# One delta-rule attention and two expert layers on one core: all pieces of a step at other places, W's expanded copies by DMA and ScalarE, two token tables

## The chip, the cores and the metric

The kernel runs on one core of one Trainium2 chip. A core has five engines that run their own instruction lists in order: TensorE (PE, matmuls; PEld is its loading of weights), VectorE (DVE), ScalarE (ACT), GpSimd (POOL) and SyncE (SP), which here only issues DMAs. They wait for one another by semaphores. Sixteen DMA engines move data between the device memory and the on-chip memory, or inside the latter. The metric is the device time of one execution in microseconds, as the median of several runs.

## The reference

```
attention (4 batches, 8 heads, 768 tokens, 48 wide), for each token t:
    y[t]   = q[t] @ state
    state += beta[t] * outer(kn[t], v[t] - kn[t] @ state)        kn = k / |k|
x   = y as [3072 tokens, 384]
x   = sum over 4 experts e:  p[:, e] * (relu(x @ w1[e]) @ w2[e])           # 384 -> 1024 -> 384, dense
out = gate * (relu(x @ v1[e*]) @ v2[e*]),  e* = the best of 8 experts for each token
```

Inputs and output are float32. The first layer needs every expert for every token, the second one expert for each token.

## The kernel before

**Numbers.** Matmuls run on pairs of 16-bit floats: a value is split into a high part (written by ACT) and a low part (the rest, by DVE or POOL), and each product is three matmuls.

**Attention** is cut into 12 steps of 64 tokens for all 32 heads (two halves x of 16 heads). In a step the keys are normed (`norm_squares` to `norm_apply`), split (`split_k`), transposed by a DMA (`turn_k`), summed into the right operand KQ (`sum_k`) and multiplied with themselves (`gram_k`) and with the queries (`gram_q`). A 32 x 32 triangular system for each head is inverted on DVE in lanes, with 31 pivots (`inverse`, lines 396 and 400), turned back (`from_lanes`) and split into TB (`split_t`, ACT L421 and DVE L422). Then come `rest` (the part of v that the state predicts), the side R, `solve_z`, `solve_y` and `solve_w`; their results, in the tile Ws, are spread with gaps into WB by `expand(0)` and `expand(1)` (line 497, four DVE copies each). `state` and `keep` update the state, `outputs` and `columns` (lines 142, 143) make the next x, transposed, in `xT`.

**Dense layer.** While attention step s runs, the dense layer works on the tokens of step s - 1. It has 16 pieces for each step; `Dense.first` (line 834; L838 and L839 make H) and `Dense.second` (line 856; after every fourth piece its sum leaves PSUM, L864 or L866). Between them are 32 **half-slots** for each step: an even one stands behind `first` of the next piece, an odd one behind `second`.

**The order by hand.** Nothing is scheduled by a tool. The tables `SLOTS` and `SECOND` (the latter for attention step 1) say in which half-slot of its dense step each piece of an attention step is written down, with negative numbers for the dense step before. `route_pieces` (the choice of the expert, half-slots 2 to 26) and `w_split` (the weights of the second layer, split and stored to the device memory image `wimg`, lines 1029 to 1033) have their own slots, and `DENSE` and `KINDS` those of the dense weights in dense step 0: a kind A, B or C says which engines split a chunk (A: ACT, ACT, POOL; B: ACT, DVE; C: ACT, POOL, POOL). Every engine gets its instructions in the order in which the half-slots are written down, and so does the SP queue with its DMAs. Two places that matter:

```python
at[16i ...]:  hidden(i + 1);  at[2 * i];  second(i);  at[2 * i + 1]      # dense piece i
SLOTS = dict(load_k=-4, norm=(-2, -1, 0, 1), ..., sum_k=(-5, -1), gram_k=(-4, 0), ..., out=27, ...)
```

So the keys of step s + 1 are loaded in half-slot 28 of one dense step and squared (L178, on ACT) in half-slot 30, two behind.

**The first step** (`begin`) has nothing to lie beside and is written down as a list of its own, before dense step 0. **Token numbers** of the tokens that go to an expert are scattered by POOL (line 1116) into one table `ids` in device memory, two scatters a step. **The sparse layer** is a tail of 27 tiles of 128 tokens: gather, transpose, `hidden` (L1295), `emit` (L1312), scatter. Its first list is read by `list_a`, and `phase_a` starts the gathers and the loads of the first three tiles' weights (L1267) in half-slot 18 of the last dense step.

Of the kernel before, what the change touches and what calls it, by code (L numbers as in the profile page):

```python
# [26 lines left out]
DENSE = dict(w=(0, 0, 1, 1, 2, 3, 3, 4, 4, 5, 6, 7, 8, 9, 10, 11, 13, 14, 15, 16, 17, 18, 20, 21, 22, 23, 24, 25, 26), r=16, t=20, e=22, c=26, i=21, p=5, load=0, keep=1)  # L27


class Attention:  # L30
# [3 lines left out]
    def __init__(self, ctx, tc, q, k, v, beta, ident, pp, xt_pool, late):  # L34
# [32 lines left out]
        self.clear(self.WB[:, 0:1])  # L67
        self.clear(self.KB0[1])
# [153 lines left out]
    def split_wide(self, s, x, low):  # L222
        KM = self.KM[:, 8 * x:8 * x + 8]
        hi, lo = (self.keys(s)[x][:, l].rearrange("p u (h c) -> p u h c", h=2)[:, :, :, 0:48] for l in range(2))
        self.nc.scalar.activation(out=hi, in_=KM, func=AF.Copy)
        low.tensor_tensor(out=lo, in0=KM, in1=hi, op=ALU.subtract)

    def split_q(self):
        self.split_q_hi()
        self.split_q_lo()  # L230

    def split_q_hi(self):
        Qv = self.Q.rearrange("p (g h) d -> p g h d", h=2)
        for h in range(2):
            self.nc.scalar.activation(out=self.QT[:, 0, :, h, 0:48], in_=Qv[:, :, h], func=AF.Copy, scale=64.0)

    def split_q_lo(self):
        nc = self.nc
        Qv = self.Q.rearrange("p (g h) d -> p g h d", h=2)
        for h in range(2):  # L240
            nc.vector.scalar_tensor_tensor(out=self.QT[:, 1, :, h, 0:48], in0=Qv[:, :, h], scalar=64.0,
                                           in1=self.QT[:, 0, :, h, 0:48], op0=ALU.mult, op1=ALU.subtract)

    def split_q_whole(self):
        nc, Q = self.nc, self.Q
# [118 lines left out]
    def split_p(self, x):  # L364
        nc = self.nc
        src = self.P32[:, 8 * x:8 * x + 8]
        nc.scalar.activation(out=self.PT[x][:, 0], in_=src, func=AF.Copy)
        self.low.tensor_tensor(out=self.PT[x][:, 1], in0=src, in1=self.PT[x][:, 0], op=ALU.subtract)
# [44 lines left out]
    def split_t(self, between=None):  # L413
        nc, TR = self.nc, self.pr
        if between:
            between()
        for q in range(4):
            b = slice(32 * q, 32 * q + 32)
            hi, lo = (self.TB[b, :, l, b].rearrange("c p (i y) -> c i p y", y=2) for l in range(2))
            src = TR[b].rearrange("c i (p y) -> c i p y", y=2)  # L420
            nc.scalar.activation(out=hi, in_=src, func=AF.Copy)  # L421
            nc.vector.tensor_tensor(out=lo, in0=src, in1=hi, op=ALU.subtract)  # L422
# [67 lines left out]
    def expand(self, f):  # L490

        for q in range(4):
            r, g, c = slice(32 * q, 32 * q + 32), q // 2, 48 * (q % 2)
            par = f ^ g
            dst = self.WB[r, :, 0:1536].rearrange("p l (u e) -> p l u e", e=96)[:, :, par:16:2, c:c + 48]
            src = self.Ws[r, par]
            self.nc.vector.tensor_copy(dst, src)
# [53 lines left out]
    def pieces(self, s):  # L551
        two = range(2)
        st = {}
# [19 lines left out]
        if s > 1:  # L573
            for x in two:
                at(P["split_k"][x], lambda x=x: self.split_k(s, x))
                at(P["turn_k"][x], lambda x=x: self.turn_k(s, x))
                at(P["sum_k"][x], lambda x=x: [self.sum_k(x, l) for l in two])
                at(P["gram_k"][x], lambda x=x: self.gram_k(x))
            at(P["split_q"], self.split_q)
# [7 lines left out]
        for n in range(4):  # L587
            f = self.expand_s if s > 1 else self.expand_d
            at(P["expand_s"][n], lambda n=n, f=f: f(*divmod(n, 2)))
        at(P["to_lanes"], lambda: self.scale_lanes(s))  # L590
# [15 lines left out]
        at(P["y"], self.save_z, self.solve_y, self.solve_yl)  # L606
        at(P["y"] + 1, lambda: self.expand(0))
        at(P["w"], self.solve_w)
        at(P["w"] + 1, lambda: self.expand(1))
# [18 lines left out]
    def begin(self, loads, parts):  # L628
        nc, two = self.nc, range(2)
        K0, K1 = self.K0, self.K1  # L630
        for x in two:
            self.blank(self.KBs[x], 2)
        loads(0)
        self.twin_beta()
        self.load_v(0)
        self.blank(self.AO, 2)
        loads(1)
        self.blank(self.TB, 4)
        loads(2)
        self.blank(self.WB[:, 1:2], 1)  # L640
        for x in two:
            self.blank(self.SB[x], 2)
        self.blank(self.KBs[2], 2)

        self.K = K0
        self.units("out", bufs=2)
        sq = self.sq = self.wk.tile([128, 16, 48], F32, name="ksq", tag="wb")
        nc.vector.tensor_tensor(out=sq, in0=K0, in1=K0, op=ALU.mult)
        self.norm_root()
        self.norm_scale()  # L650
        rm = self.norm_heads(nc.vector, self.r0)
        for x in two:
            self.norm_wide(nc.vector, K0, x, rm)
        for x in two:
            self.split_wide(0, x, nc.vector)
        for x in two:
            for l in two:
# [877 lines left out]
```

## Time and profile before

| | us |
|---|---|
| median of 3 runs (lowest, highest) | 1322.87 (1321.1, 1325.64) |
| the profiled execution | 1319.7 |
| its span, first to last instruction | 1317.9 |
| first step of attention, alone | 0 to 61.3 |
| dense step 0 | 61.3 to 173.6 |
| dense steps 1 to 9 | 173.6 to 954 |
| dense steps 10 and 11 | 954 to 1090 |
| tail of 27 tiles | 1090 to 1318 |

| engine | busy us | share of the span |
|---|---|---|
| PE | 1149.0 | 87% |
| PEld | 880.9 | 67% |
| DVE | 840.1 | 64% |
| ACT | 638.7 | 48% |
| POOL | 450.4 | 34% |

How to read the rows below: a row of a view of windows gives, for a stretch, its length, for each engine the busy time (and number of instructions), then the granted TensorE clock (1.00 is 2.4 GHz, 0.50 is 1.2 GHz), the mean busy share of the DMA engines and their GB/s. A row of waits says who waited for whom: total us, times, longest. A row of the timeline has the start, the length, the engine, the line and the tiles, and in brackets the idle time before it and what ended that. A row of groups has the busy time, the mean ns of one, and the idle time before.

### The profile page before, as it was taken

The numbers are of one execution on the slowest core, as the hardware profiler recorded it, in microseconds if no ns is written. First come the engines' busy times: TensorE is split into PE (matmuls) and PEld (weight loads), VectorE is DVE, ScalarE is ACT, GpSimd is POOL, SyncE is SP. The second block draws the span as 40 slices with busy tenths as digits, with TensorE's granted clock in tenths as the row PEclk, the third lists the DMA queues.
The fourth block names the chain that finished last, engine by engine and source line by source line (L and its number), as shares of the span: only waits on it lengthen the run. The fifth ranks groups of instructions, "written<-read, shape, count | busy, mean of one in ns | idle before, by whom it ended". The sixth has DMA issues, their size and how long they took to land. (4 is left out here: it accounts for less than half of the span.)

```text
span 1317.9 us, 32914 instructions
## 1 busy us (share of the span) xinstructions
PE 1149.0 (87%) x12906; PEld 880.9 (67%) x12906; DVE 840.1 (64%) x2898; ACT 638.7 (48%) x1248; POOL 450.4 (34%) x436
## 2 busy tenths in 40 slices
PE   3477699798798898988988979879899999999997
PEld 3355577566576676766766757657677777878876
DVE  8776778588577676886776768767777344212221
ACT  6665655355464455555554646555564314222221
POOL 5466732332334224323243233423441022222221
PEclk8688999999899899999998999989999999999999
DMA  9981244725524446254364463444532157796960
GB/s 224 220 194 17 45 99 115 104 66 137 81 64 117 81 115 105 71 132 87 91 108 80 128 116 90 113 81 121 113 94 73 25 157 230 247 282 181 342 171 27
DMA packets 249504, 163.00 MB, mean 124 GB/s; under 512 B 196271, under 2 KB 230908, under 8 KB 249344
## 3 DMA queue, kind: packets, MB, share of 16 engines
q1 hardware_dynamic: 243600, 150.77, 48.6%
q0 software_dynamic: 4656, 9.87, 2.4%
q8 instruction: 104, 1.70, 0.6%
q14 instruction: 56, 0.46, 0.1%
q10 hardware_dynamic: 1088, 0.20, 0.1%
HBM read 142.52 MB, written 35.80 MB: 135 GB/s over the span
## 5 line engine op out<-in xcount | busy, mean ns | idle before, releaser
L856 PEld LDWEIGHTS <-H 128*128 128x128 f16 x2304 | 224.9, 100 | 217.6 <-issue 44.1
L856 PE MATMUL po<-W,H 128*128 128x384 f16 x1728 | 324.2, 338 | 50.9 <-ACT H L838 37.1
L834 PE MATMUL ph<-xT,W 128*128 128x256 f16 x2808 | 336.3, 275 | 7.5 <-POOL W L819 6.0
L834 PEld LDWEIGHTS <-W 128*128 128x128 f16 x2808 | 272.7, 99 | 52.5 <-POOL W L819 7.4
L839 DVE SCALAR_TENSOR_TENSOR H<-ph,H 128x512 f16<-128x512 f32 x192 | 131.5, 688 | 161.9 <-ACT H L838 160.8
L1031 POOL TENSOR_TENSOR wso<-wst,wso 128x768 f16<-128x768 f32 x64 | 105.1, 1642 | 281.6 <-ACT wst L1030 259.7
L838 ACT ACTIVATE H<-ph 128x512 f16<-128x512 f32 x192 | 112.7, 592 | 154.3 <-PE ph L834 153.3
L1300 DVE SCALAR_TENSOR_TENSOR H<-ph,H 128x512 f16<-128x512 f32 x54 | 37.2, 690 | 151.3 <-ACT H L1299 151.3
L856 PE MATMUL po<-Wlate,H 128*128 128x384 f16 x576 | 102.6, 332 | 18.5 <-DVE acc L866 18.5
L1295 PEld LDWEIGHTS <-slot 128*128 128x128 f16 x1944 | 110.7, 98 | 3.8 <-issue 0.5
L1295 PE MATMUL ph<-xt,slot 128*128 128x128 f16 x1944 | 113.1, 219 | 0.2 <-DMA xt<-g 0.2
L400 DVE TENSOR_TENSOR tt<-tt,pr 128x60 f32<-128x60 f32 (+34 forms) x660 | 110.7, 210 | 0.7
L1312 PE MATMUL po<-slot,H 128*128 128x384 f16 x648 | 110.0, 326 | 0.6 <-DVE H L1300 0.6
L396 DVE TENSOR_TENSOR pr<-tt,KQ 128x60 f32<-128x60 f32 (+34 forms) x660 | 108.4, 202 | 0.8
L1312 PEld LDWEIGHTS <-H 128*128 128x128 f16 x648 | 62.1, 98 | 39.1 <-DVE H L1300 0.9
L1317 POOL DMA_INDIRECT out_dram<-ob,idx x27 | 27.3, 1011 | 166.6 <-ACT ob L1316 129.6
L834 PE MATMUL ph<-xT,Wlate 128*128 128x256 f16 x648 | 78.8, 276 | 3.8 <-ACT Wlate L815 2.5
L215 POOL TENSOR_TENSOR KB<-Kr,KB 32x384 f16<-32x384 f32 x80 | 76.7, 958 | 5.8 <-ACT KB L214 1.3
L362 POOL TENSOR_TENSOR AO<-O,AO 32x256 f16<-32x256 f32 x48 | 32.8, 684 | 128.7 <-ACT AO L361 126.7
L1029 ACT ACTIVATE wso<-wst 128x768 f16<-128x768 f32 x64 | 53.3, 833 | 44.1 <-DMA wimg<-wso 42.1
L834 PEld LDWEIGHTS <-Wlate 128*128 128x128 f16 x648 | 61.6, 99 | 12.7 <-ACT Wlate L815 2.9
L1299 ACT ACTIVATE H<-ph 128x512 f16<-128x512 f32 x54 | 32.2, 597 | 77.0 <-PE ph L1295 75.6
(308 smaller groups left out, 1615.2 us busy)
## 6 DMA issues: line engine op xcount, KB each, us to landing
slot<-wimg SPq DMA_DIRECT2D x108, 768.0 KB
wst<-in_moe_w_dram SPq DMA_DIRECT2D x65, 384.0 KB
wimg<-wso SPq DMA_DIRECT2D x64, 384.0 KB
xb<-xr SPq DMA_DIRECT2D x48, 98.0 KB
Qr<-in_q_dram SPq DMA_DIRECT2D x24, 192.0 KB
Vr<-in_v_dram SPq DMA_DIRECT2D x96, 48.0 KB
W<-in_moe_w_dram SPq DMA_DIRECT2D x11, 384.0 KB
Kr<-in_k_dram SPq DMA_DIRECT2D x84, 48.0 KB
```

The lines of the kernel that those rows point to most:

```text
L215: self.low.tensor_tensor(out=KB[r, 1, :, 64 * h:64 * h + 48], in0=src, in1=hi, op=ALU.subtract)
L396: nc.vector.tensor_tensor(out=p, in0=t[:, :, j:j + 1].to_broadcast([128, m, j]), in1=AT[:, j, 0:j].unsqueeze(1).to_broadcast([128, m, j]), ...
L400: nc.vector.tensor_tensor(out=t, in0=t, in1=p, op=ALU.subtract)
L834: nc.tensor.matmul(ph[:, i], w1[:, a, k, 128 * i:128 * i + 128], xT[:, b, k], start=(n == 0), stop=(n == 8))
L838: nc.scalar.activation(out=H[:, 0], in_=ph, func=AF.Relu)
L839: nc.vector.scalar_tensor_tensor(out=H[:, 1], in0=ph, scalar=0.0, in1=H[:, 0], op0=ALU.max, op1=ALU.subtract)
L856: nc.tensor.matmul(po[t], H[:, a, i, 128 * t:128 * t + 128], w2[:, b, i], start=(f == 0 and i == 0 and n == 0), stop=(f == 3 and i == 1 an ...
L1029: self.nc.scalar.activation(out=o[:, 0], in_=t, func=AF.Copy, scale=scale)
L1031: self.nc.gpsimd.tensor_tensor(out=o[:, 1], in0=t, in1=o[:, 0], op=ALU.subtract)
L1295: nc.tensor.matmul(ph[:, i], w[:, a, k, 128 * (i % 2):128 * (i % 2) + 128], xt[:, 3 * b + k], start=(m == 0), stop=(m == 8))
L1300: nc.vector.scalar_tensor_tensor(out=H[:, 1], in0=ph, scalar=0.0, in1=H[:, 0], op0=ALU.max, op1=ALU.subtract)
L1312: nc.tensor.matmul(po, H[:, a, i], w[:, b, i % 2], start=(q == 0 and i == 0 and m == 0), stop=(q == 1 and i == 3 and m == 2))
```

## The change

What is computed stays. Other places (half-slots) for nearly every piece, other engines for some, and a second table:

- The tables `SLOTS` and `SECOND`, `DENSE`, `KINDS` (with a kind D: all on POOL), the slots of the routing pieces and of `w_split` are replaced.
- `expand(0)` of steps 1 to 11 is done by eight DMAs from the SP queue, `expand(1)` by four ScalarE copies. The state's expanded copies `SB` go by DMA for half 0 (two DMAs for each of two pieces) and stay on ACT for half 1.
- The low part of the keys of half 1 moves from POOL to DVE.
- `begin` becomes a list of named pieces in the order of the text `ORDER`.
- The two scatters of a step go to a table each; `list_a` gathers from both, and `list_b` takes the smaller number.
- `phase_a` moves from half-slot 18 to 21 of the last dense step.

```diff
-SLOTS = dict(load_k=-4, norm=(-2, -1, 0, 1), split_k=(-10, -7), turn_k=(-8, -5), sum_k=(-5, -1), gram_k=(-4, 0), to_lanes=1, split_g=(1, 2), split_q=-4, turn_q=-3, gram_q=(5, 6), split_p=(6, 7), expand_s=(8, 10, 12, 14), init=2, pivots=(2, 3, 3, 2, 2, 3, 3, 3, 3, 3, 2, 2), from_lanes=14, split_t=15, rest=(16, 17), z=19, y=21, w=23, state=25, keep=25, out=27, load_q=16, load_v=23)
-SECOND = dict(SLOTS, to_lanes=0, split_g=(8, 10), gram_q=(9, 10), split_p=(11, 12), expand_s=(5, 6, 7, 8), init=1, pivots=(2, 2, 3, 2, 3, 2, 3, 2, 3, 2, 3, 2, 2), from_lanes=14, split_t=15, rest=(12, 15), z=17, y=19, w=21, state=23, keep=23, out=25, load_k=0, load_q=16, load_v=22, norm=(13, 15, 18, 18))
-HEAD = dict(loads=(2, 5, 7, 15, 23))
-KINDS = "AAABABACABACABACABACBACBABCABABA"
+SLOTS = dict(load_k=-6, load_q=16, load_v=36, norm=(2, 2, 3, 4), split_k=(-24, -7), turn_k=(-14, -5),
+             sum_k=(-5, -1), gram_k=(-2, 0), to_lanes=0, scale=0, split_g=(1, 4), split_q=(-4, -4), turn_q=0,
+             gram_q=(5, 6), split_p=(8, 7), expand_s=(8, 10, 12, 14), init=5, pivots=(4, 6, 3, 3, 5, 5, 2, 3, 0),
+             from_lanes=13, split_t=15, rest=(15, 17), z=19, save=19, y=21, e0=22, w=24, e1=24, state=25, keep=25,
+             out=28)
+SECOND = dict(load_k=0, load_q=18, load_v=34, norm=(14, 17, 17, 18), split_k=(-14, -7), turn_k=(-11,
+              -7), sum_k=(-5, -1), gram_k=(-2, 0), to_lanes=0, scale=1, split_g=(7, 11), split_q=(-4, -4), turn_q=-3,
+              gram_q=(9, 10), split_p=(12, 13), expand_s=(4, 3, 7, 8), init=1, pivots=(4, 0, 4, 0, 4, 1, 4, 4, 1, 2,
+              5, 2), from_lanes=13, split_t=15, rest=(10, 16), z=17, save=17, y=19, e0=25, w=21, e1=22, state=24,
+              keep=26, out=30)
+ROUTE = dict(first=(0, 4, 7, 9, 9, 10, 10), rest=(2, 6, 11, 16, 20, 24, 27))
+WAYS = dict(e0="S", e1="A", sb="SSAA", apply="V", klow="PV")
+WSLOTS = dict(back=0, six=(7, 10, 13, 18, 20, 27), seven=(4, 7, 11, 13, 18, 20, 27))
+HEAD = dict(loads=(2, 4, 7, 14, 21))
+KINDS = "AAADABABABBBABBAABAABAACCABCABBBB"
...
+ORDER = """
+cq cw ck0 zk1 load0 twin zk0 ck1 v0 za load1 zt zs0 zk2 load2 zw units square root scale square1 heads wide0 wide1
...
+out1 columns sum110
+"""
...
@@ split_k
-            self.low.tensor_tensor(out=KB[r, 1, :, 64 * h:64 * h + 48], in0=src, in1=hi, op=ALU.subtract)
+            low = self.nc.gpsimd if WAYS["klow"][x] == "P" else self.nc.vector
+            low.tensor_tensor(out=KB[r, 1, :, 64 * h:64 * h + 48], in0=src, in1=hi, op=ALU.subtract)
@@ expand
-            self.nc.vector.tensor_copy(dst, src)
+            if how == "S":
+                for l in range(2):
+                    self.nc.sync.dma_start(out=dst[:, l], in_=src[:, l])
+            elif how == "A":
+                self.nc.scalar.activation(out=dst, in_=src, func=AF.Copy)
@@ route_pieces
-                    out=self.ids.rearrange("a (b c) -> (a b) c", c=1),
+                    out=self.ids[t].rearrange("a (b c) -> (a b) c", c=1),
@@ main
-    six, seven = (8, 11, 14, 17, 20, 29), (4, 8, 11, 14, 17, 20, 29)
+    six, seven = WSLOTS["six"], WSLOTS["seven"]
-    at[last + 18].append(phase_a)
+    at[last + 21].append(phase_a)
```

## Rows read from the trace of the kernel before

**Rows 1.** Windows: stretch, PE, PEld, DVE, ACT, POOL busy, clock, DMA share, GB/s.
```profile
0.00:61.30 61.30, 21.25 (x321) 18.87 (x322) 50.32 (x197) 40.50 (x68) 35.99 (x62) 0.72 0.98 221
61.30:173.60 112.30, 87.80 (x894) 62.69 (x894) 77.10 (x235) 67.44 (x120) 67.38 (x54) 0.88 0.46 94
173.60:954.00 780.40, 687.85 (x7766) 523.04 (x7764) 578.35 (x2007) 419.32 (x818) 262.63 (x238) 0.97 0.47 101
954.00:1028.00 74.00, 72.00 (x795) 55.53 (x793) 55.37 (x209) 37.73 (x71) 22.04 (x20) 1.00 0.29 82
1090.00:1318.00 228.00, 218.83 (x2648) 174.70 (x2646) 55.15 (x170) 60.69 (x147) 54.02 (x53) 0.99 0.70 209
```

**Rows 2.** Waits of PE in 173.6:954: us in total, times, longest.
```profile
PE po L856 <- ACT H L838: 37.1, 8, 7.4
PE ps L296 <- DVE KQ L289: 20.4, 9, 2.3
PE po L856 <- DVE acc L866: 16.0, 9, 1.8
PE psz L429 <- ACT R L450: 7.7, 9, 0.9
PE psz L429 <- DVE R L453: 5.5, 9, 0.6
```

**Rows 3.** Windows: the first of nine half-clock stretches, and the nine's sum.
```profile
262.30:269.10 6.80, 2.76 (x9) 1.15 (x10) 3.77 (x10) 4.21 (x11) 0.51 (x1) 0.50 0.65 155
...
sum 47.60, PE 35.11 PEld 16.58 DVE 34.53 ACT 27.79 POOL 8.37; mean PE 3.90 PEld 1.84 DVE 3.84 ACT 3.09 POOL 0.93
```

**Rows 4.** Waits of PE in 61.3:173.6 (dense step 0): the two longest of twelve.
```profile
PE po L856 <- ACT TB L421: 6.1, 1, 6.1
PE ph L834 <- POOL W L819: 6.0, 4, 2.3
```

**Rows 5.** Timeline of ACT, SP and DVE around the end of dense step 5.
```profile
698.67 0.84 ACT L178 ACTIVATE ksq<-Kr 128x768 f32<-128x768 f32 x1 [7.27 <-DMA Kr<-in_k_dram]
...
685.38 2.15 SPq L272 DMA_TRANSPOSE KTB<-KB  x1
687.58 6.43 SPq L155 DMA_DIRECT2D Kr<-in_k_dram  x8
...
693.71 0.76 DVE L289 TENSOR_TENSOR KQ<-KTB 128x512 f16<-128x512 f16 x2 [1.71 <-DMA KTB<-KB]
```

**Rows 6.** Timeline of DVE in half-slots 22 and 23 of dense step 5.
```profile
667.91 3.43 DVE L497 COPY WB<-Ws 32x768 f16<-32x768 f16 x4
671.37 1.14 DVE L866 SCALAR_TENSOR_TENSOR acc<-po,p,acc 128x384 f32<-128x384 f32 x2
```

**Rows 7.** Groups of the whole span: busy us, mean ns of one, idle before.
```profile
L396 DVE TENSOR_TENSOR pr<-tt,KQ 128x60 f32<-128x60 f32 (+34 forms) x660 | 108.4, 202 | 0.8
L400 DVE TENSOR_TENSOR tt<-tt,pr 128x60 f32<-128x60 f32 (+34 forms) x660 | 110.7, 210 | 0.7
L839 DVE SCALAR_TENSOR_TENSOR H<-ph,H 128x512 f16<-128x512 f32 x192 | 131.5, 688 | 161.9 <-ACT H L838 160.8
L422 DVE TENSOR_TENSOR TB<-pr,TB 32x512 f16<-32x512 f32 x44 | 40.7, 926 | 15.6 <-ACT TB L421 14.6
L215 POOL TENSOR_TENSOR KB<-Kr,KB 32x384 f16<-32x384 f32 x80 | 76.7, 958 | 5.8 <-ACT KB L214 1.3
L500 ACT ACTIVATE SB<-SC 64x768 f16<-64x768 f16 x40 | 33.4, 835 | 0.5
```

**Rows 8.** SP issues of SB's copies, and windows of and after them.
```profile
90.59 9.92 SPq L504 DMA_DIRECT2D SB<-SC  x8
...
102.00:104.00 2.00, 2.00 (x17) 1.46 (x16) 1.01 (x9) 1.44 (x3) 2.00 (x2) 1.00 0.00 0
```

**Rows 9.** Timeline of SP and PE: first tile's weights issued, first matmuls.
```profile
1072.87 2.34 SPq L1267 DMA_DIRECT2D slot<-wimg  x4
...
1092.87 2.17 PE L1295 MATMUL ph<-xt,slot 128*128 128x128 f16 x36
```

More of the change, by code (lines that the diff above doesn't have):

```diff
@@ L648, in begin @@
[L648 to L656, printed above, removed]
-            for l in two:
-                self.turn_k_first(0, x, l)
-            for l in two:
-                self.sum_k(x, l)
-        ps = [self.gram_d(x) for x in two]
@@ L714, in begin @@
-        self.inverse(0, 15, 31)
-        self.from_lanes(0)
-        self.split_t(lambda: self.side_lo(R, 0))
-        self.split_q()
-        self.turn_q()
-        gate = self.cp.tile([128, 1], F16, name="gate")
-        nc.gpsimd.tensor_copy(gate, self.TB[:, 15, 1, 127:128])
-        xT = self.xt_pool.tile([128, 2, 3, 256], F16, name="xT")
-        self.solve_z()
-        for x in two:
-            self.split_p(x)
-        parts(1)
-        self.save_z()
-        self.sum_k(0, 0)
-        self.solve_y()
@@ L730, in begin, with step @@
-        parts(2)
-        self.solve_yl()
-        self.load_v(1)
-        loads(4)
-        self.expand(0)
-        self.sum_k(0, 1)
-        self.solve_w()
-        self.expand(1)
-        parts(3)
-        self.gram_k(0)
-        pv = [self.outputs(0, x) for x in two]
-        self.columns(pv, xT)
-        self.sum_k(1, 0)
-        self.sum_k(1, 1)
-        return xT
+        done = defaultdict(int)
+        st = {}
+        steps = {}
+        def step(name, f):
+            steps[name] = f
@@ new lines, in begin, with square @@
+        step("zt", lambda: self.blank(self.TB, 4))
+        step("zw", lambda: self.blank(self.WB[:, 1:2], 1))
+        step("twin", self.twin_beta)
+        step("v0", lambda: self.load_v(0))
+        step("v1", lambda: self.load_v(1))
+        step("q1", lambda: self.load_q(1))
+        for i in range(5):
+            step(f"load{i}", lambda i=i: loads(i))
+        def square():
+            self.K = K0
+            sq = self.sq = self.wk.tile([128, 16, 48], F32, name="ksq", tag="wb")
+            nc.vector.tensor_tensor(out=sq, in0=K0, in1=K0, op=ALU.mult)
@@ new lines, in begin, with pivot @@
+        step("lanes", self.to_lanes)
+        step("lscale", self.scale_first)
+        step("qscale", lambda: nc.scalar.activation(out=self.Q, in_=self.Q, func=AF.Copy, scale=64.0))
+        step("side", lambda: setattr(self, "R", self.side("R", 0)))
+        step("sidelo", lambda: self.side_lo(self.R, 0))
+        def pivot():
+            j = done["pivot"]
+            if j == 0:
+                self.TS, self.pr = (t.bitcast(F32).rearrange("p (c i) -> p c i", c=16) for t in self.lent)
+            self.inverse(0, j, j + 1)
+            done["pivot"] += 1
@@ new lines, in z @@
+        def z():
+            st["xT"] = self.xt_pool.tile([128, 2, 3, 256], F16, name="xT")
+            self.solve_z()
+        step("z", z)
+        step("save", self.save_z)
+        step("y", self.solve_y)
+        step("ylo", self.solve_yl)
+        step("w", self.solve_w)
+        step("gk0", lambda: st.__setitem__("gk", self.gram_d(0)))
+        step("gk0o", lambda: self.gram_o(0, st["gk"]))
+        step("columns", lambda: self.columns([st["pv", x] for x in two], st["xT"]))
+        for n in range(3):
+            for i, f in enumerate(parts[n]):
+                step(f"W{n}{i}", f)
@@ L746, in state_first @@
+        for name in ORDER.split():
+            steps[name]()
+        return st["xT"]
     def state_first(self):
@@ L1363 @@
     sparse.setup_b(sp, dense.ap)
-    xT0 = attn.begin(head_loads, head_parts)
-    attn.low = nc.gpsimd
+    xT0 = attn.begin(head_loads, parts)
     at = defaultdict(list)
@@ L1375 @@
     for s in range(NS - 1):
-        for o, g in zip((2, 6, 11, 14, 19, 24, 26) if s < NS - 2 else (1, 3, 6, 9, 9, 10, 10), sparse.route_pieces(s, dense)):
+        for o, g in zip(ROUTE["rest"] if s < NS - 2 else ROUTE["first"], sparse.route_pieces(s, dense)):
             at[32 * (s + 1) + o].append(g)
@@ L1406 @@
         at[slots[n]].append(lambda n=n: w_split(n))
+        at[slots[n] + WSLOTS["back"]].append(lambda n=n: w_store(n))
     lists, tiles, cols = {}, {}, {}
```

296 lines of the change are left out of this document (162 added, 134 removed).

## The prediction

> **What bounds the kernel now.** I read the windows first, one for each stage [rows 1]. The tail is matmul work almost without a gap (218.83 us busy of 228.00), and dense step 10 has PE busy for 72.00 of 74.00: little to win there. In the first step alone PE is busy for 21.25 of 61.30 us and DVE for 50.32; that is a chain of small pieces. In dense steps 1 to 9 PE is busy for 687.85 of 780.40 us, so 92.5 us are idle, and in dense step 0 for 87.80 of 112.30. PE is thus the engine that the dense loop goes by, and what can be won is its idle time and its half-clock time.
>
> Second, the waits of PE in steps 1 to 9 [rows 2]. Five rows make 86.7 us of the 92.5: for H at the step's end 37.1 us (8 of 9 steps), for `sum_k` 20.4, for po's copy out of PSUM 16.0, for R ahead of `solve_z` 7.7 and 5.5. Each comes once a step, so one place in the order sets it, and that is what the change moves.
>
> Third, the clock [rows 3]. In nine stretches, 47.60 us together, the granted clock is 0.50, 1.2 GHz of 2.4, and PE is busy for 35.11 us of them. The longest begin where PE had just idled for H: in the first, PE works for 2.76 of 6.80 us. Half of the busy time there is lost, 17.6 us. So steps 1 to 9 lose 92.5 + 17.6 = 110.1 us, 12.2 each, and without loss a step takes (780.4 - 110.1) / 9 = 74.5 us, 2.33 for a half-slot.
>
> **The change, part by part.** I take the profiled execution, 1319.7 us, and what each part gives in its stage.
>
> *Keys squared later (end of step, 37.1 us).* At the end of step 5 ACT stood for 7.27 us at the squares, until the keys' DMA landed, with two H copies behind it in its list [rows 5]. SP had ended the issue of that load at 694.01, and it landed 4.66 us later. The change issues the load in half-slot 26 and squares in half-slot 2 of the next step, eight half-slots or 18.6 us later. Issue (6.43) and landing (4.66) make 11.1, so 7.5 us cover what SP waits beforehand, and the wait goes. What is late next: the load now stands ahead of half 1's `turn_k` in the SP queue, and `gram_k` of half 1 at the step's start needs `turn_k`'s result by way of `sum_k`, with H behind that on DVE. `turn_k` landed 6.2 us after its issue (685.38 + 2.15 to 693.71), and PE's nine waits for `sum_k` [rows 2], one a step, are those for half 0, so half 1 had slack. Eight loads ahead of it cost up to 6.43 us, and the stores of xb, until now ahead of it, go behind it. Left: 0 to 2 us a step, I take 0.8, since DVE writes the keys' low parts earlier than POOL did.
>
> *`sum_k` of half 0 (20.4 us).* It stood behind `columns` on DVE. Now it is written one half-slot before `outputs`, and its `gram_k` comes two half-slots later than before. The wait goes; nothing new stands there, as half 0's transpose has moved from half-slot 24 to 18.
>
> *W's expanded copies (16.0 us).* Four DVE copies took 3.43 us ahead of po's copy, 1.14 [rows 6], and PE waited 1.8 for it. DVE loses both sets. Four ScalarE copies replace `expand(1)`, each like SB's 835 ns [rows 7], 3.3 us a step, where ACT would wait for the state; ACT is busy for 419.32 of 780.40 us. The state's lower half goes to DMA and gives ACT 1.7 back. `expand(0)` becomes eight DMAs on SP. The nearest rows are SB's eight, with twice the pieces: 9.92 us to issue, and from 102 the DMA engines stand still [rows 8]. `outputs` comes six half-slots, 14 us, after; the bounds are 0 and, behind a store that waits for POOL, 3 us a step. With z, y and w at their new places I put down 0.7.
>
> *POOL to DVE.* Four low parts of 958 ns [rows 7] leave POOL. On DVE I bound them by TB's row, 926 ns for 512 elements, so 0.7 for 384, and by POOL's 958: 2.8 to 3.8 us a step, less than the copies that DVE loses. In that half-slot POOL still makes the state's low parts. The Trainium skill (SBUF — State Buffer, on the shared port pair) says that a VectorE instruction with two SBUF inputs and a GpSimd one that reads SBUF exclude each other for a whole instruction. By that rule two POOL instructions of nearly 1 us would hold DVE up for some 1.8 us a step, an estimate from the rows, and the sum would be 16 us higher; the rows show TB's DVE halves at 926 ns beside POOL work, and the sum goes by them.
>
> *Pivots squeezed.* An inverse is at most (108.4 + 110.7) / 11 = 19.9 us of DVE a step, and an H 0.69 [rows 7]. Until now it had 12 half-slots (28 us) for 19.9 + 6 x 0.69 = 24; now 8 (18.6 us) for 19.9 + 4 x 0.69 = 22.7. DVE falls up to 4.1 us behind. From the inverse to z there is one half-slot more (2.3 us), so R is up to 1.8 us later than now, when PE waits 13.2 / 9 = 1.5 us for it [rows 2]. Bounds 0 and 3.3 a step; I take 2.0, because half of `rest` moves up.
>
> *Steps 1 to 9 together.* Left are 0.8 + 0.7 + 2.0 and 0.4 for the clock, 3.9 us a step, 35 in all. Gain 110.1 - 35 = 75 us.
>
> *Dense step 0.* Idle 24.5 us; the clock 0.88 takes 13.5, of which, by the share of rows 3 (35.11 / 47.60), 10 fall on working time: 34.5 lost. The longest waits [rows 4] are one of 6.1 us, for TB with the inverse late, and four for POOL's low parts. The new kinds have three chunks C for six, thirteen B for ten: POOL loses some 8 us of its 67.38 [rows 1], DVE gets three more chunks and loses the expansions. DVE has the longer list now in the first half; I leave 8 us for it. `outputs` at half-slot 30, one dense piece before the next step, adds 2.5 that is not there now, the clock 3, the rest 5. Gain 34.5 - 18.5 = 16 (bounds 0 and 30).
>
> *Without effect.* The first step alone: its list keeps DVE's chain, and some pieces fill gaps, 0 (from -2 to +2). Two tables end POOL's wait for its own scatter, but PE waits for none of it. `phase_a` three half-slots later: the first weights are issued 20.0 us before their first matmul [rows 9], 14 are left for four DMAs of 768 KB, 15 us at the tail's mean of 209 GB/s, which counts its idle times [rows 1]; 0, at most 3. Dense step 10: 1.
>
> The sum: 1319.7 - 75 - 16 - 1 = 1227.7 us for the profiled execution. The median of the runs shown is 3.2 us above that execution, so 1231 for the median.
>
> **Rivals.**
> *DVE becomes the bound.* The pivots stay 4 us behind, R waits 5 us a step, and after such a wait the clock falls as in rows 3, 1.7 more. For: DVE is busy for 578.35 us of 780.40 now, 64 a step, some 62 of 78 after. Against: `rest` and the splits behind the inverse have not grown. It takes 6.7 for 2.4, 39 us: 1270.
> *All waits go.* Only 1 us a step is left (26 us better) and dense step 0 loses 8.5 less: 1197. For: every moved piece has slack by the rows; against: so many lists seldom fit.
> *Slower: `turn_k` behind the key load.* The eight loads wait for DVE's low parts, these for ACT's four expansions (3.3), state copies and high parts. Then `turn_k` is issued some 8 us later and lands, at 6.2, about 8 us after PE wants `gram_k`, and H stands behind `sum_k` on DVE; with a half-clock stretch of 10 us behind it (5 lost) that is 13 a step for the 12.2 that go now, and the other waits still left. It decides from a landing 6 us late. Steps 1 to 9 then take 9 x (74.5 + 13 + 2) = 806, 25 more than now, and step 0 gains nothing: 1348. Against: ACT has nothing else there now.
> *It doesn't do what it says.* The squares still wait, for a buffer, with the 37 us and most of their clock: 1285.
>
> **How the numbers follow.** Forecast 0.60 (1205 to 1255), DVE bound 0.15, all waits gone 0.14, squares still late 0.06, slower 0.05. Two in ten outside: 1192 to 1288. A measurement of this kernel tells 0.3%, 4 us, from no change: faster 0.93, same 0.02, slower 0.05.
>
> **What would show it.** Right: no wait of ACT at L178, rows for `sum_k` and po gone, the clock near 1.00 in steps 1 to 9, steps of 77 to 80 us. Wrong: PE waits for R or H above 4 us a step (pivots), for `gram_k` at the step's start (the SP queue), for WB at L538 (the DMA copies), or POOL still the longest wait in step 0.

## The result, and the profile after

The changed kernel takes 1203.31 us (median of 4 runs, 1199.66 to 1208.4), the kernel before in the same measurement 1323.83 (1321.1 to 1325.64): a ratio of 0.9094, with a 95% interval of 0.9052 to 0.9136. The prediction was 1231, its range 1192 to 1288. The profiled execution is the slowest of the four, 1208.4 us with a span of 1206.7; it stands against the 1227.7 of the prediction's sum. One of the four runs of the kernel called "w_split's slots undone" below had a granted clock of 0.747 where the others had 0.97, and took 1467.76 us; its row gives the median of the other three.

The windows of the changed kernel by stage, columns as in [rows 1]: length, busy time (instructions) of PE, PEld, DVE, ACT and POOL, clock, DMA share, GB/s:

```profile
0.00:60.70 60.70, 22.44 (x320) 20.09 (x321) 48.83 (x198) 39.01 (x66) 37.39 (x63) 0.72 1.00 218
60.70:154.00 93.30, 81.35 (x889) 60.44 (x889) 75.27 (x230) 65.42 (x113) 55.18 (x46) 0.93 0.54 115
154.00:840.50 686.50, 667.40 (x7767) 518.98 (x7766) 549.29 (x1974) 436.98 (x840) 244.34 (x202) 1.00 0.56 119
840.50:911.50 71.00, 71.00 (x792) 55.34 (x791) 52.86 (x201) 41.31 (x78) 22.22 (x23) 1.00 0.51 98
977.60:1206.60 229.00, 217.50 (x2630) 174.62 (x2628) 54.86 (x169) 59.24 (x144) 55.02 (x54) 0.98 0.72 212
```

Against [rows 1], dense steps 1 to 9 gave 780.4 - 686.5 = 93.9 us, dense step 0 19.0, dense step 10 3.0 and the first step 0.6. The tail's matmuls ran from 1092.87 to 1317.9 before and run from 977.59 to 1206.7 now, 4.0 us longer, and dense step 11 takes 1.2 more. The sum is 111.3 us, the difference of the spans 111.2. PE now idles for 19.1 us in steps 1 to 9, where it idled for 92.5.

PE's waits in steps 1 to 9 of the changed kernel (us in total, times, longest), to be read against [rows 2]:

```profile
PE ps L312 <- DVE KQ L305: 11.5, 7, 3.0
PE po L922 <- DVE H L905: 2.0, 5, 0.5
PE po L922 <- DVE acc L932: 1.6, 3, 0.7
PE psz L457 <- DVE R L481: 1.1, 5, 0.2
```

The 37.1 us for H from ACT are gone, the acc row fell from 16.0 to 1.6, the two R rows from 13.2 to 1.1. The first row has the name of the old wait for `sum_k`, but it is another one: the old stood at half 0, in half-slot 28; this one is at half 1, where a new step begins. Only two half-clock stretches are left there, and PE works through both (their sum follows). The kernel before has ten: [rows 3] left out one of 3.4 us at 948.4.

```profile
sum 6.80, PE 6.78 PEld 4.09 DVE 4.82 ACT 4.03 POOL 0.73; mean PE 3.39 PEld 2.04 DVE 2.41 ACT 2.02 POOL 0.36
```

Timeline of ACT, SP and DVE at the end of dense step 3, which answers to [rows 5] (those, like [rows 6], are from dense step 6, counted from 0, not 5 as they were called):

```profile
397.05 0.84 ACT L199 ACTIVATE ksq<-Kr 128x768 f32<-128x768 f32 x1
...
375.20 3.79 SPq L176 DMA_DIRECT2D Kr<-in_k_dram  x8
379.09 4.24 SPq L288 DMA_TRANSPOSE KTB<-KB  x1
...
372.26 2.90 DVE L238 TENSOR_TENSOR KB<-Kr,KB 32x384 f16<-32x384 f32 x4 [2.26 <-ACT KB L236]
...
389.17 0.76 DVE L305 TENSOR_TENSOR KQ<-KTB 128x512 f16<-128x512 f16 x2 [5.46 <-DMA KTB<-KB]
```

ACT's squares have no bracket: the keys, whose issue ended at 378.99, were there 18 us later. On SP the key load now stands ahead of half 1's `turn_k`, whose issue ends at 383.33. DVE stood 5.46 us until the transpose had landed, and PE behind it for 3.0.

### The profile page after: what moved, and what is told of

Same layout as the page of the kernel before. It is cut to its first block, busy times and chain, and to the rows that moved or that the text cites. A ratio compares the mean times of both kernels' runs of the same rounds, so it can differ in the third digit from the quotient of the medians.

```text
span 1206.7 us, 33186 instructions
## 1 busy us (share of the span) xinstructions
PE 1125.0 (93%) x12906; PEld 877.8 (73%) x12906; DVE 807.1 (67%) x2859; ACT 656.7 (54%) x1268; POOL 422.2 (35%) x394
## 5 line engine op out<-in xcount | busy, mean ns | idle before, releaser
L922 PEld LDWEIGHTS <-H 128*128 128x128 f16 x2304 | 221.4, 98 | 138.1 <-issue 6.5
L922 PE MATMUL po<-W,H 128*128 128x384 f16 x1728 | 308.7, 328 | 5.1 <-DVE H L905 3.0
L421 DVE TENSOR_TENSOR tt<-tt,pr 128x60 f32<-128x60 f32 (+34 forms) x660 | 111.3, 209 | 0.7
L378 POOL TENSOR_TENSOR AO<-O,AO 32x256 f16<-32x256 f32 x48 | 47.0, 980 | 161.7 <-ACT AO L377 159.7
L1385 PEld LDWEIGHTS <-H 128*128 128x128 f16 x648 | 62.1, 98 | 38.3
L1389 ACT ACTIVATE ob<-po,sm 128x384 f32<-128x384 f32 x27 | 15.7, 580 | 81.4 <-PE po L1385 81.3
```

Source lines behind the costliest of these rows:

```text
L378: self.low.tensor_tensor(out=lo, in0=src, in1=hi, op=ALU.subtract)
L421: nc.vector.tensor_tensor(out=t, in0=t, in1=p, op=ALU.subtract)
L922: nc.tensor.matmul(po[t], H[:, a, i, 128 * t:128 * t + 128], w2[:, b, i], start=(f == 0 and i == 0 and n == 0), stop=(f == 3 and i == 1 an ...
L1385: nc.tensor.matmul(po, H[:, a, i], w[:, b, i % 2], start=(q == 0 and i == 0 and m == 0), stop=(q == 1 and i == 3 and m == 2))
```

## The experiments

Steps 1 to 9 are measured here from the first H of dense step 1 to the first H of dense step 10: 780.2 us in the kernel before, 686.8 in the changed one. "Undone" means one part of the change taken back, "alone" one part done in the kernel before. Every time stands beside a run of the kernel before on the same chip (medians 1322.14, 1322.47 and 1326.05 in the three sets), so the ratios are what compares across sets. The last column is from one profiled execution of each kernel. The changed kernel's four executions differ by 8.7 us, and a kernel that was altered in dense step 0 alone ("kinds undone") is 5.0 us shorter in steps 1 to 9, so a difference of some 5 us in that column shows nothing by itself.

| kernel | median us | ratio to before (95%) | steps 1 to 9 |
|---|---|---|---|
| squares undone | 1264.0 | 0.9568 (0.953, 0.9606) | 738.6 |
| copies undone | 1205.39 | 0.9109 (0.9079, 0.9139) | 687.8 |
| gram_k undone | 1212.9 | 0.9178 (0.9149, 0.9207) | 690.6 |
| inverse and rest undone | 1223.6 | 0.9266 (0.9233, 0.9299) | 700.2 |
| low parts alone | 1332.53 | 1.0083 (1.0055, 1.0111) | 781.2 |
| w_split's slots undone | 1242.08 | 0.9432 (0.9382, 0.9482) | 724.1 |
| kinds undone | 1211.73 | 0.9176 (0.9139, 0.9212) | 681.8 |
| load behind, phase_a at 18 | 1189.48 | 0.8993 (0.8969, 0.9016) | 669.3 |
| squares alone | 1303.41 | 0.9836 (0.9805, 0.9866) | 762.1 |
| copies alone | 1317.27 | 0.994 (0.992, 0.996) | 767.5 |
| copies undone, low parts beside | 1242.26 | 0.9366 (0.9331, 0.9401) | 716.1 |
| half 1's low parts undone | 1232.26 | 0.9292 (0.9262, 0.9323) | 707.4 |

**The squares.** Undone:

```diff
-SLOTS = dict(load_k=-6, ..., norm=(2, 2, 3, 4), ...
+SLOTS = dict(load_k=-4, ..., norm=(-2, -1, 0, 1), ...
```

> The changed kernel with the key load and the four pieces of the norm back at their old half-slots (28, and 30 to 1); all else stays. Theory (the squares' wait for the keys' DMA held up H at the end of each step, and PE's clock fell behind it): the rows for H come back, about 4 us a step in nine steps, 37 us, and half-clock stretches with 10 to 15 us: 1240 to 1255 us. Rival (ACT has become lighter or SP earlier, so that the old place would do now): within 10 us of the changed kernel, 1200 to 1213.

It costs 51.8 us in steps 1 to 9, and the median is 9 us above the expected range. PE's longest wait there, and the timeline of ACT and SP at the end of dense step 5:

```profile
PE po L922 <- ACT H L904: 59.3, 8, 9.6
```

```profile
573.53 0.84 ACT L199 ACTIVATE ksq<-Kr 128x768 f32<-128x768 f32 x1 [9.42 <-DMA Kr<-in_k_dram]
...
563.57 8.13 SPq L176 DMA_DIRECT2D Kr<-in_k_dram  x8
```

The load takes 8.13 us to issue where it took 6.43 [rows 5], and ends 1.8 us before the squares run. The theory holds, and the old place is worse in the new order than it was in the old one: half-clock stretches begin at the end of eight steps. The wait for half 1's `sum_k`, 11.5 us in the changed kernel, is gone here, since the load stands behind `turn_k` again.

The same part alone in the kernel before:

> The kernel before with one edit: the key load two half-slots later... that is in half-slot 26 for 28, and the norm's four pieces in half-slots 2 to 4 of the next dense step for 30 to 1. Theory (this wait and the clock behind it stand by themselves): PE's 37.1 us for H at the step's end go, with most of the 17.6 us lost at half clock; the other waits stay: 45 to 55 us less, 1270 to 1277. Rival (a gap removed turns into the next wait of the same step, as the run with only the low parts moved showed): 20 to 35 us less, 1288 to 1302, with larger waits for R, for acc or for H on DVE.

(The load stands in half-slot 26, two earlier, and the squares eight half-slots later than in the kernel before.) The rival's number was right: 22.6 us less at the median, 18.1 of them in steps 1 to 9. Its reason was so in part only. PE's waits there:

```profile
PE ps L296 <- DVE KQ L289: 30.2, 15, 2.3
PE po L856 <- DVE acc L866: 16.0, 9, 1.8
PE po L856 <- DVE H L839: 12.3, 20, 1.5
```

The 37.1 us are gone. The waits for R and acc, which the rival expected to grow, are what they were; a wait for DVE's H is new, and `sum_k` rose by 9.8. That rise is a price of the edit itself. Half 0's nine waits are still 20.4 us; the six new ones are for half 1, at the start of a step, as in the changed kernel, for the load stands ahead of half 1's `turn_k` here too. Timeline of SP and DVE at the end of dense step 2:

```profile
333.10 3.78 SPq L155 DMA_DIRECT2D Kr<-in_k_dram  x8
...
339.83 3.51 SPq L272 DMA_TRANSPOSE KTB<-KB  x1
...
347.64 0.76 DVE L289 TENSOR_TENSOR KQ<-KTB 128x512 f16<-128x512 f16 x2 [5.08 <-DMA KTB<-KB]
```

POOL had written the last low part at 333.07; the transpose was issued 6.8 us later.

**W's copies.** Undone:

```diff
-WAYS = dict(e0="S", e1="A", sb="SSAA", apply="V", klow="PV")
+WAYS = dict(e0="V", e1="V", sb="SSAA", apply="V", klow="PV")
```

> The changed kernel with both sets of W's expanded copies back on DVE. Theory (DVE's four copies stand ahead of po's copy out of PSUM and PE waits 1.8 us for it in each step; DMAs and ScalarE do them beside other work): PE's wait for acc is back at some 16 us, 1216 to 1224. Rival 1 (the two sets are 6.9 us of DVE a step, and with the pivots squeezed DVE falls behind: R or H waits grow too): above 1235. Rival 2 (with outputs one half-slot later and the pieces behind it moved, DVE has the room): 1200 to 1210.

Rival 2 by the time: 1.0 us in steps 1 to 9, and a median 2.1 us higher, within the intervals. Eight copies are on DVE again, and PE's wait for acc is 5.3 us, not 16. The timeline of DVE, which answers to [rows 6], says why (the rival's reason, the later place, was not tried by itself):

```profile
597.07 1.43 DVE L529 COPY WB<-Ws 32x768 f16<-32x768 f16 x4
598.53 1.14 DVE L932 SCALAR_TENSOR_TENSOR acc<-po,p,acc 128x384 f32<-128x384 f32 x2
```

The same four copies take 1.43 us where they took 3.43. In the kernel before POOL was writing the low parts of the next keys at that moment, and a low part of the second layer's weights while TB was split. These are POOL's rows of the kernel before, which the prediction does not show:

```profile
649.57 1.64 POOL L1031 TENSOR_TENSOR wso<-wst,wso 128x768 f16<-128x768 f32 x1 [5.83 <-ACT wst L1030]
...
666.93 4.19 POOL L215 TENSOR_TENSOR KB<-Kr,KB 32x384 f16<-32x384 f32 x4
```

So I took every DVE instruction of a line and split them by whether a POOL instruction overlapped it. In the kernel before, a copy of W takes 350 ns in the 54 cases without one, and some 973 ns in 27 of the 36 beside `L215` (the first of each set of four takes 460, and six more beside other POOL work differ); a low part of TB takes 684 ns in 37 cases, some 1745 in the ten beside `L1031`, and 1507 in one more. The range of each line shows it (times, then ns least/median/most), in the kernel before:

```profile
L422 DVE TENSOR_TENSOR TB<-pr,TB x44: 671/686/1749, 120.8 to 996.8; 32x512 f16<-32x512 f32 x44
...
L453 DVE SCALAR_TENSOR_TENSOR Y<-Vr,Y x12: 557/1742/1745, 49.9 to 1009.3; 128x384 f16<-128x384 f32 x12
```

and in the changed kernel, where no low part of TB from dense step 0 on meets a POOL instruction:

```profile
L450 DVE TENSOR_TENSOR TB<-pr,TB x44: 669/682/692, 106.8 to 881.5; 32x512 f16<-32x512 f32 x44
```

The change also moved the split of half 0's keys (half-slot 22 to 8) and `w_split` (out of half-slot 14). Three kernels test what that did. First, the low parts back beside DVE's copies:

```diff
-             ... split_k=(-24, -7), turn_k=(-14, -5),
+             ... split_k=(-10, -7), turn_k=(-8, -5),
-WAYS = dict(e0="S", e1="A", ...
+WAYS = dict(e0="V", e1="V", ...
```

> The changed kernel with both sets of W's copies on DVE, and besides the low parts of half 0's keys on POOL back in half-slot 22 beside the first set (transpose in 24). Theory (POOL's low parts hold each copy of the first set for some 0.6 us): the first set takes 3.4 us a step again, PE's wait for acc rises from 5.3 to 14 to 18 us, the time from 1205 to 1214 to 1222. Rival (the wait was the copies' alone): acc's wait stays near 5 us, 1202 to 1209.

PE's wait for acc in steps 1 to 9:

```profile
PE po L922 <- DVE acc L932: 23.1, 10, 2.6
```

The theory holds, with more than its numbers: 27 of its 88 copies take some 974 ns, each beside POOL's low parts, and the wait rose by 17.8 us against the run with the copies alone undone. The time rose by more than the wait, 37 us between the medians and 34 by the ratios. Steps 1 to 9 are 28.3 us longer: 17.8 of the wait for acc, 7.5 of waits of PE at the outputs that the profile puts down to issue, 4.1 less for `sum_k`, and 7.2 of PE's busy time, with the clock falling in seven stretches for three. The tail is 3.7 longer; the rest, and what the transpose's old place adds, is not settled.

Second, the copies to DMA and ScalarE alone in the kernel before (from dense step 0 on):

```diff
-            self.nc.vector.tensor_copy(dst, src)
+            if not getattr(self, "ways", False):
+                self.nc.vector.tensor_copy(dst, src)
+            elif f:
+                self.nc.scalar.activation(out=dst, in_=src, func=AF.Copy)
+            else:
+                for l in range(2):
+                    self.nc.sync.dma_start(out=dst[:, l], in_=src[:, l])
```

> The kernel before with one edit: from attention step 1 on W's first expanded set by eight DMAs on SP, its second by four ScalarE copies, in their old half-slots. The prediction's term: PE's 16.0 us for acc go, 12 to 16 us less, 1307 to 1311. Rival (as where only the low parts moved away from the copies: acc's wait goes, and PE then meets the next link of DVE's list, or the DMAs' queue): acc's wait goes, the time stays within 4 us of the kernel before.

Between the two: 8.8 us (5.3 to 10.6 by the interval). The acc row is gone. Of its 16.0 us, 12.7 show up in steps 1 to 9; the wait for H at the step's end rises from 37.1 (eight steps) to 41.3 (nine), and dense step 0 is 3.1 longer.

Third, the low parts away from the copies, alone in the kernel before. This kernel splits step 2's keys ahead of their norm; the instructions are the same, so it serves for the timing alone.

```diff
-SLOTS = dict(load_k=-4, norm=(-2, -1, 0, 1), split_k=(-10, -7), ...
+SLOTS = dict(load_k=-4, norm=(-2, -1, 0, 1), split_k=(-24, -7), ...
```

> The kernel before with one edit: the split of the keys of half 0 (the low parts on POOL) moves from half-slot 22 to 8; W's copies stay on DVE at 22 and 24. Theory (a DVE copy of W takes 350 ns alone and 973 ns where POOL writes a key's low part at the same time; this, not the copies as such, made PE wait for po's copy): the set in half-slot 22 falls from 3.43 to 1.4 us, PE's wait for acc from 16.0 us to about 5, and the time by 8 to 12 us, to 1311 to 1315. Rival (the copies' number counts): acc's wait stays at 16, within 3 us of the kernel before.

Both missed: the theory named what goes, and not the time. The copies do fall to 350 ns and acc's wait is gone, but nothing is won: steps 1 to 9 take 1.0 us more, and dense step 0 8.8 more. PE's waits in steps 1 to 9:

```profile
PE po L856 <- ACT H L838: 33.3, 9, 7.2
...
PE po L856 <- DVE H L839: 14.8, 17, 1.5
PE lg L1067 <- DMA xtr<-xr: 7.8, 9, 1.6
```

The 16 us came back as two new waits, for DVE's H behind TB's low parts (3.9 us, one of them held up) and for a transpose of x on the SP queue. The conflict was the cause of the acc wait; taking it away alone pays nothing, because the next links of the same step are as late.

**gram_k of half 0.** Undone:

```diff
-             sum_k=(-5, -1), gram_k=(-2, 0), ... out=28)
+             sum_k=(-5, -1), gram_k=(-4, 0), ... out=27)
```

> The changed kernel with gram_k of half 0 back in half-slot 28 and the outputs in 27. Theory (sum_k stood behind the outputs' columns on DVE, with gram_k too close behind it): PE's wait for sum_k of 2.3 us a step is back, 1218 to 1226. Rival (the wait was not set by the order on DVE but by the transpose DMA of half 0, which now comes six half-slots sooner): 1200 to 1210.

PE's waits in steps 1 to 9:

```profile
PE ps L312 <- DVE KQ L305: 16.8, 12, 1.7
```

The theory's wait is back in all nine steps, at 1.5 us for 2.3; half 1's, the other three times, is smaller than in the changed kernel. Steps 1 to 9 lose 3.8 us, the median 9.6, of which the profiled execution shows 4.1; 1212.9 lies between the two ranges. Why the wait is shorter than 2.3 was not tried. One thing differs: in the kernel before two small instructions ahead of `columns` on DVE (lines 1101 and 1105) took 0.82 and 0.74 us beside POOL's low parts of half 1's keys, and here, with these on DVE, 0.17 each.

**The inverse and rest.** Undone:

```diff
-             ... init=5, pivots=(4, 6, 3, 3, 5, 5, 2, 3, 0), from_lanes=13, ... rest=(15, 17), ...
+             ... init=2, pivots=(2, 3, 3, 2, 2, 3, 3, 3, 3, 3, 2, 2), from_lanes=14, ... rest=(16, 17), ...
```

> The changed kernel with the inverse in twelve half-slots from 2 on, from_lanes in 14 and rest in 16 and 17, as before. The prediction held that squeezing the inverse into fewer half-slots would put R 2.0 us a step later; the changed kernel shows 0.1. Theory 1 (the wait for R goes by the place of rest and from_lanes alone, the squeeze costs nothing): with the old places the waits for R are back at 1.0 to 1.5 us a step, 1212 to 1218. Theory 2 (R stood behind other work of DVE, the expansions and POOL's parts, that has left): the wait stays near 0, 1200 to 1208.

Neither as stated, and slower than both: the squeeze with the places behind it is a gain, 13.4 us in steps 1 to 9. R's waits are 0.5 us a step, between the theories, but acc waits too:

```profile
PE po L922 <- DVE acc L932: 10.0, 6, 2.9
...
PE psz L457 <- DVE R L481: 4.3, 7, 0.6
```

DVE's timeline in dense step 7 of this kernel, and then in the changed one:

```profile
656.71 0.28 DVE L421 TENSOR_TENSOR tt<-tt,pr 128x8 f32<-128x8 f32 x2
660.11 0.69 DVE L905 SCALAR_TENSOR_TENSOR H<-ph,H 128x512 f16<-128x512 f32 x1 [3.12 <-ACT H L904]
660.72 0.74 DVE L429 SCALAR_TENSOR_TENSOR TS<-tt,bl 128x256 f32<-128x256 f32 x2
...
662.13 1.10 DVE L932 SCALAR_TENSOR_TENSOR acc<-po,p,acc 128x384 f32<-128x384 f32 x2
```

```profile
651.47 0.27 DVE L421 TENSOR_TENSOR tt<-tt,pr 128x8 f32<-128x8 f32 x2
651.68 0.76 DVE L429 SCALAR_TENSOR_TENSOR TS<-tt,bl 128x256 f32<-128x256 f32 x2
...
654.28 0.69 DVE L905 SCALAR_TENSOR_TENSOR H<-ph,H 128x512 f16<-128x512 f32 x1 [1.09 <-ACT H L904]
```

With twelve half-slots DVE has finished the pivots and stands 3.12 us for ScalarE's H (1.1 to 3.9 in the nine steps), and only then turns the inverse back; po's copy stands behind that. With `from_lanes` one half-slot earlier the turn fills the time before H. The four places were moved back together, so what each gives is not shown.

**w_split's slots.** Undone:

```diff
-WSLOTS = dict(back=0, six=(7, 10, 13, 18, 20, 27), seven=(4, 7, 11, 13, 18, 20, 27))
+WSLOTS = dict(back=0, six=(8, 11, 14, 17, 20, 29), seven=(4, 8, 11, 14, 17, 20, 29))
```

> The changed kernel with the pieces that split the second layer's weights (POOL's 1.64 us low part among them) back at the old half-slots. Theory (in half-slot 14 POOL's low part makes one of TB's four low parts on DVE take 1.75 us for 0.68, and R comes later by it): PE's wait for R rises from 1.1 us to 5 to 12 in steps 1 to 9, the time by 4 to 12 us, 1207 to 1215. Rival (R's wait went because from_lanes stands one half-slot earlier, right behind the last pivot): the time within 3 us of the changed kernel although TB's row is slow again.

The slow TB is back (11 of 48, ten of them at 1.74 us or more), and the cost is three times the most I expected, 37.3 us in steps 1 to 9, but not at R. PE's waits:

```profile
PE po L922 <- DVE H L905: 22.8, 18, 3.0
PE po L922 <- ACT H L904: 11.9, 9, 2.4
...
PE psz L457 <- DVE R L481: 1.1, 5, 0.2
```

Timeline of DVE, POOL and ACT in dense step 5:

```profile
520.49 3.89 DVE L450 TENSOR_TENSOR TB<-pr,TB 32x512 f16<-32x512 f32 x4 [1.34 <-ACT TB L446]
...
520.04 1.64 POOL L1098 TENSOR_TENSOR wso<-wst,wso 128x768 f16<-128x768 f32 x1 [4.64 <-ACT wst L1097]
...
511.91 0.84 ACT L1096 ACTIVATE wso<-wst 128x768 f16<-128x768 f32 x1 [5.40 <-DMA wimg<-wso]
```

Two things come together. TB takes 3.89 us, with H behind it on DVE, so PE waits for H and not for R. And in half-slot 11 ScalarE stands 5.40 us for the last store of the weights, with H behind it: all those waits of ACT are 70.2 us here and 39.7 in the changed kernel.

**The kinds of dense step 0.** Undone:

```diff
-KINDS = "AAADABABABBBABBAABAABACCABCABBBB"
-DENSE = dict(w=(0, 0, 1, 1, 1, 2, 3, 3, 3, 5, 6, 7, 7, 9, 10, 11, 13, 15, 15, 15, 16, 17, 20, ...
+KINDS = "AAABABACABACABACABACBACBABCABABA"
+DENSE = dict(w=(0, 0, 1, 1, 2, 3, 3, 4, 4, 5, 6, 7, 8, 9, 10, 11, 13, 14, 15, 16, 17, 18, 20, ...
```

> The changed kernel with the old kinds and half-slots for the dense weights' splits in dense step 0 (six chunks C, ten B). Theory (POOL's low parts were the longest list of step 0, 67.38 us before and 55.18 after): PE's waits for W come back by some 6 us and step 0 takes 99 to 104 us for 92.7; 1210 to 1215. Rival (step 0 gained from the other moves, the inverse and TB above all): step 0 within 3 us, 1200 to 1207.

(The new table has 32 letters, fourteen of them B; the section on the change prints an A too many, and the prediction counted thirteen B.) The theory: step 0, from first H to first H, takes 101.1 us for 92.7, though PE's waits for the weights' parts are only 2.6 us longer (7.2 for 4.6) and acc's make 4.1 more. (Steps 1 to 9 are 5 us shorter here, with 7.9 us of waits for `sum_k`; the changed kernel's profiled execution, the slowest of its four, has 11.5.)

**Half 1's low parts.** The rule that the next text calls the page's is that of the Trainium skill (SBUF — State Buffer, on the shared port pair).

```diff
-WAYS = dict(e0="S", e1="A", sb="SSAA", apply="V", klow="PV")
+WAYS = dict(e0="S", e1="A", sb="SSAA", apply="V", klow="PP")
```

> The changed kernel with the low part of half 1's keys back on POOL. The page's rule on the shared port pair, which the prediction weighed, is what the trace of the changed kernel shows where both sides read the state memory: nine of the forty low parts on DVE take 1158 ns for 552 beside POOL's low parts of the state. Theory (half 1's transpose is on the path to the step's start by way of sum_k; on POOL the low parts stand behind the state's low parts and take 0.96 for 0.72 us each, so the transpose comes 2 to 3 us later): PE's wait for sum_k of half 1 rises from 11.5 to 25 to 35 us, 1215 to 1228. Rival (the key load ahead of it on the SP queue sets it alone): within 4 us of the changed kernel.

The theory: 20.6 us in steps 1 to 9, the median 4 us beyond its range, the wait a little short of it. POOL takes 4.16 us for four and starts them after the state's low parts, and the wait doubles. It grew by 11.3 us; PE's busy time grew by 9.9, at a clock of 0.98 in steps 1 to 9 where it was 1.00:

```profile
PE ps L312 <- DVE KQ L305: 22.8, 8, 4.5
```

**The key load behind the transpose, and phase_a.**

```diff
-SLOTS = dict(load_k=-6, ...
+SLOTS = dict(load_k=-5, ...
-    at[last + 21].append(phase_a)
+    at[last + 18].append(phase_a)
```

> The changed kernel with two edits that the trace tells apart, by stretches. First, the key load one half-slot later, 27, so that half 1's transpose stands ahead of it on the SP queue: PE's wait for sum_k of half 1, 11.5 us in steps 1 to 9, goes, and the rest of the half-clock time; the squares, seven half-slots behind, still don't wait: 9 to 13 us less there. Second, phase_a back in half-slot 18: the tail takes 225 us again for 229.1, 4 less. Sum: 1186 to 1192. Rival for the first (the transpose waits for the low parts, not for the queue): steps 1 to 9 unchanged, 1198 to 1201. Rival for the second (the tail is longer for another reason): the tail stays at 229.

This is the fastest kernel, 1189.48 us (1187.16 to 1190.35), by 0.8993 / 0.9094 = 0.989 of the changed kernel's time. Steps 1 to 9 take 17.5 us less, for 9 to 13 expected; some of it is the changed kernel's profiled execution, its slowest (between the medians it is 13.8 in all). Timeline of SP and DVE at the end of dense step 3:

```profile
370.74 1.94 SPq L288 DMA_TRANSPOSE KTB<-KB  x1
372.72 4.49 SPq L176 DMA_DIRECT2D Kr<-in_k_dram  x8
...
367.77 2.90 DVE L238 TENSOR_TENSOR KB<-Kr,KB 32x384 f16<-32x384 f32 x4 [2.26 <-ACT KB L236]
...
379.13 0.75 DVE L305 TENSOR_TENSOR KQ<-KTB 128x512 f16<-128x512 f16 x2
```

and PE's longest wait in steps 1 to 9, where no row for `sum_k` is left:

```profile
PE po L922 <- DVE acc L932: 2.4, 4, 1.0
```

The transpose is issued 0.1 us after its last low part instead of 3.9 after, and DVE no longer waits. The whole window of steps 1 to 9 has a clock of 1.00 and no half-clock stretch. phase_a gave less than expected: the tail is 3.1 us shorter (226.0), but dense step 11, from its first H to the tail's first matmul, is 1.6 longer (64.2 for 62.6). With phase_a at 21 the tail of the other kernels took 224.9 to 235.1 us, so the place is not shown to set it.

## Why the prediction was right, and where its sizes were off

The time lies inside the stated range and below the forecast's own (1205 to 1255). The waits that the change was to remove are gone; of what was to be left, two were wrongly reasoned (the keys' low parts beside POOL and the pivots), and that of W's copies came out well by luck in part. Of the signs named, a step of 76.3 us lies just under the 77 to 80.

*The squares* (37.1 us): right. The load's issue and landing fit into the eight half-slots, and undoing it brings back 59.3 us of waits.

*What is late next at the step's start*: the mechanism was named, the key load ahead of half 1's `turn_k`. I took 0.8 us a step; it is 11.5 / 9 = 1.3, and the last experiment removes it. It is also the mechanism of the slower rival, at a tenth of the price given there: the loads' issue ended 3.8 us after DVE's low parts, and `turn_k` was that much late, not 8.

*W's copies* (16.0 us, 0.7 a step left): the wait went (0.2 left), but the reason was half of it. "Four DVE copies took 3.43 us ahead of po's copy" was a fact of the neighbour, POOL's low parts, and their move out of half-slot 22 does as well as DMAs and ScalarE in the new order. That the term came out was luck in part: the change made both moves.

*The rule on the shared port pair* (the Trainium skill, SBUF — State Buffer): here the step failed. The prediction set the rule aside because TB's rows stood at 926 ns "beside POOL work" [rows 7]. That is a mean of 684 ns without and 1745 with a POOL instruction beside it. The trace agrees with the rule: a held DVE instruction comes to its end only after the POOL instruction beside it, 0.2 us (a copy of W) to 0.54 us (a low part of TB) behind, and the pivots, which are not held, take their first input from PSUM (last section). The price that I worked out by it, 1.8 us a step for the keys' low parts, was too high, since nine of these forty are held, by 0.6 us each: 0.6 a step. And the rule worked for the change, at places that I had not looked at: TB's low parts no longer lie beside POOL's, nor would the first set of copies. It also made new cases: the product that norms the keys (line 225) now takes 1.35 us beside POOL for 0.95, and the copy of Ws (line 504) 0.92 for 0.36.

*Pivots squeezed* (2.0 us a step left, from 0 to 3.3): the mis-sized term. R's wait is 1.1 / 9 = 0.1. The price of an inverse, 19.9 us, was too high. It added the busy times of two lines whose instructions overlap on DVE (the next begins before the last has ended). Together they hold DVE for 15.7 us in the kernel before and for 15.5 in the changed one, as the windows of the instructions on `tt` show for one inverse each (length, DVE busy, clock, DMA share, GB/s):

```profile
621.70:644.85 23.15, 15.67 (x120) 1.00 0.21 57
...
634.00:651.72 17.72, 15.51 (x121) 1.00 0.58 151
```

15.7 + 4 x 0.69 = 18.5 us fit into the 18.6 of eight half-slots, so DVE does not fall behind. In the kernel before it stood still for some 4 us of these 23, for ScalarE's H; now it stands for 0.1 of 17.7.

*The clock* (0.4 a step): right, half of 6.78 us in nine steps is 0.4.

*The sum of steps 1 to 9*: forecast 3.9 us left a step above a floor of 74.5. Measured: idle 19.1 / 9 = 2.1 and the clock 0.4, above (667.4 - 3.4) / 9 = 73.8. 1.4 + 0.7 a step, times nine, are the 18.9 us that were missing. The tenth half-clock stretch makes 0.2 of the floor's 0.7; the rest of it is not explained. The result lies between the forecast and the rival *all waits go* (1 us left, 1197), 1.7 us below the forecast's own range.

*Dense step 0*: 19.0 for 16. The kinds make 8.4 of it; the wait for TB gave way to one of 4.9 us for R, and the rest was not tried by itself. *Tail*: a loss of 4.0 for 0, with a gather that lands late (4.0 us of waits at `xt`). *Dense step 10*: 3 for 1.

What the prediction did not see: the waits don't add up one by one. It summed five rows of waits, and the sum was short by a fifth (75 for 93.9). Done alone in the kernel before, squares, copies and low parts give 18.1, 12.7 and -1.0 us of steps 1 to 9, where their rows say 37.1 and, for the same wait, 16.0 twice; part of the squares' shortfall is the edit's own price at `turn_k`. Undone one by one, six parts cost 51.8, 37.3, 20.6, 13.4, 3.8 and 1.0, 127.9 in all for a gain of 93.4.

## What to carry to other kernels

Before a mean duration is used as a price, look at its least and most: two values far apart are two situations, and here what another engine did beside the slow ones told them apart. Before two lines' busy times are added, see whether their instructions overlap. A row of waits says what a wait is worth only if nothing of the same step is as late behind it; in a tight order a move made alone can pay little, and one undone alone shows what it holds. When a load is moved ahead on a queue, look at what now stands behind it: here one half-slot back took away 11.5 us of waits.

## What the runs showed of the hardware that I had not expected

In these traces a DVE copy or two-input instruction that takes its inputs from the on-chip state memory is held where it starts while POOL is subtracting there: a 16-bit copy of 32x768 takes 973 ns for 350, a subtraction of 32x512 1745 for 684, one of 128x384 1742 for 558 and one of 32x384 1158 for 552. Small ones are held too: beside line 215 a product of 128x16 takes 817 ns for 174 and a conversion of 128x2 743 for 168. Each ends its own time less some 0.14 us after the POOL instruction has ended (the copy 0.21, the subtraction of 32x512 0.54), so the price depends on how much of POOL's instruction is left.

Not held is what takes its first input from PSUM: H takes 687 ns alone and 689 beside POOL, and the pivots 198 and 206. The pivots' `tt` is a tile of the PSUM pool (`units`, line 375 of the kernel before). A 32x32 transpose on DVE (line 411) takes 711 ns either way.
